# A fused attention and GLU block: scores three steps ahead, more buffers, sums stored in read order, and the A22 products later in a unit

## The chip, the cores and the metric

One core of a Trainium2 chip runs the whole program; seven cores are idle. The time is the device time of one execution in microseconds. Matrix products run on TensorE (PE in the profile), its weight loads are listed as PEld; VectorE is DVE, ScalarE is ACT, GpSimd is POOL. SyncE (SP) issues nearly all DMAs, one behind the other, from one queue in the program's order: a DMA that waits for its data holds up all that stand behind it.

## The reference

```python
mod = (_silu(c) @ w_mod).reshape(c.shape[0], 6, 1, -1)
sa, ca, ga, sb, cb, gb = (mod[:, 0], ..., mod[:, 5])
h = _layernorm(x, axis=-1) * (1 + ca) + sa
# attention: 2048 queries, 32 heads of 128, 16 pairs of key and value heads, the last 512 keys
q = (h @ wq).reshape(B, Sq, Hq, Dh)...
scores = jnp.einsum("bhqd,bhkd->bhqk", q, k) * (Dh ** -0.5)
p = _softmax(scores, axis=-1)
o = jnp.einsum("bhqk,bhkd->bhqd", p, v)
x = x + ga * (o.reshape(B, Sq, Hq * Dh) @ wo)
h = _layernorm(x, axis=-1) * (1 + cb) + sb
# gated unit: 576 -> 4608 -> 576
x = x + gb * ((_sigmoid(h @ w_gate) * (h @ w_up)) @ w_down)
```

All tensors are float32, x is 2048 x 576. Each float32 operand is split into a high part and a remainder (hi, lo), and a product is the sum of three: hi*lo, lo*hi and hi*hi.

## The kernel before, in words

The program has three stages: the Q phase (x @ wq), the attention, and what follows (output product and gated unit). The first two are one loop over steps n from -224 to 520. In a step it calls what was registered for it (`at_n`: ahead of the step's main work, `at_late`: behind it), and then the main work. In both stages every engine executes its instructions in the order in which this loop issues them.

**Q phase**, n = -224 to -1. The product is done by a seven-product scheme for 2 x 2 blocks. A unit u (32 of them) is one weight block; its seven products are named A11, A12, A22, S1, S2, S4, S3, each 7 matmuls of 128 x 512. `order` is the list of products by step and `place` its inverse. A11 and A12 of the first 14 units (EARLY) stand ahead of all; after that come five products for each early unit and seven for each later one. TensorE adds S2, S3 and A22 of a unit into the bank PA[u] (tag a, two buffers), S1 and S4 into PC[u] (tag c, one buffer). Between, ScalarE copies a bank (to gate, gate1, b), and VectorE adds such a copy to a bank to make an output (qo). So A22 of a unit can't start before VectorE has read PA[u] for the output of S3, S3 not before ScalarE has copied S2's result out (gate), and A11 of the unit after next not before A22's output has left the bank. `load_raw` fetches a unit's weights (two buffers RAW), `w_sums` builds sums on GpSimd (ws), `raw_hi`/`sum_hi` and `split_lo` the hi and lo parts (sw; sa is A22's alone) on ScalarE and VectorE. q goes to DRAM (qscr). `convert` makes the x operands of the second half. A planner places the preparation of the later stages' weights (jobs "ab", "tail", "wo", "down": loads, sums, splits, stores of x, xr, wsc, dsc, wosc) by the costs in its last line.

**Attention**, n = 0 to 511, a step for each tile of 128 queries; four tiles are a block b (one head, 512 queries), two blocks a unit of output, four units a group (one key head: two halves of the queries by two heads). In step n TensorE makes the scores of tile n + 2 (st), a quarter of the product with V for the block five steps back (ot), and the transposes of tile n's exponentials (pt). VectorE takes the negated row maximum of st (neg), ScalarE the exponential (pp) with its row sum; ScalarE copies pt (ptt, hi part) and VectorE takes the remainder (ptt, lo part). When a block's four exponentials are done, VectorE inverts the sums (rs), SP writes them to DRAM (`put_rs`, rscr<-rs), reads them back as a row for all partitions (`get_rs`, rb<-rscr), and `ov_out` multiplies ot by them into an O buffer (ov), ten steps after the block's start. `put_o` stores a unit's O buffer. For 16 of the 32 heads in the second half GpSimd adds planes of two units first (`sum_o`, `sum_last`, tile sx), and their stores come 15 and 19 steps after the last exponential instead of 9.

```python
1310         b, i = divmod(n - 5, TPB)
1314         if 0 <= n + 2 < N:
1315             scores(n + 2)
1316         if ok(b):
1317             pv(b, i)
1318         if 0 <= n < N:
1319             transp(n)
1320         if 0 <= n + 2 < N:
1321             expo(n + 2)
```

Most instructions are issued through one helper, so the profile's rows carry its line (L36); they are told apart by their tiles.

Of the kernel before, what the change touches and what calls it, by code (L numbers as in the profile page):

```python
# [9 lines left out]
F32 = mybir.dt.float32  # L10
# [6 lines left out]
P = 128  # L17
BLK = 512
TPB = BLK // P
# [25 lines left out]
def adaln_block_kernel(ctx: ExitStack, tc: tile.TileContext, x, k_cache, v_cache, wq, wo, w_gate, w_up, w_down,  # L45
                       c, w_mod, out):
    early = [True]
    nc = Ordered(tc, early, tc.nc)
    S, D = x.shape[1], x.shape[2]
    HKV, SK, DH = k_cache.shape[1], k_cache.shape[2], k_cache.shape[3]  # L50
# [3 lines left out]
    W = min(4096, max(256, SK // 4))  # L54
# [9 lines left out]
    NBLK = NB * H  # L64
# [5 lines left out]
    dram = ctx.enter_context(tc.tile_pool(name="dram", bufs=1, space=bass.MemoryType.DRAM))  # L70
# [6 lines left out]
    pools = {}  # L77
# [25 lines left out]
    def keep_order(i):  # L103
        if held[0]:
            tc.keep_in_program_order(i)
# [185 lines left out]
    NLO = -NQ  # L291
    EARLY = 14
# [36 lines left out]
    def w_hi(key, src, n=2):  # L329
        t = sw_tile([P, 5, 2, P]) if n == 2 else qw.tile([P, 5, 1, P], F32R, tag="sa", name="sa", bufs=2)  # L330
        nc.scalar.activation(t[:, 0:3], src, AF.Copy)
        HALF[key] = t, src
# [20 lines left out]
        w_hi((u, k), RAW[(u + 1) % 2][:, :, 0::2, :] if k == 2 else RAW[(u + 1) % 2][:, :, 3:4, :], 2 if k == 2 else 1)  # L353

    def sum_hi(u, k):
        w_hi((u, k), WS.pop((u, k)))

    def split_lo(u, k):
        w_lo((u, k), u, ((S1, S2), (S4, S3), (A11, A12), None, (A22,))[k])
# [180 lines left out]
    def at_n(n, fn, *args):  # L540
        at_step.setdefault(n, []).append((fn, args))
# [8 lines left out]
    for u in range(EARLY):  # L550
        order += [(u, A11), (u, A12)]
    for u in range(2 * HKV):
        if u >= EARLY:
            order.append((u, A11))
            order.append((u - 1, A22))
            order += [(u, a) for a in (S1, A12, S2, S4, S3)]
        else:
            order.append((u, S1))
            if u:
                order.append((u - 1, A22))  # L560
            order += [(u, a) for a in (S2, S4, S3)]
    order.append((2 * HKV - 1, A22))
    assert len(order) == NQ
    place = {x_: q_n(i) for i, x_ in enumerate(order)}
# [5 lines left out]
    for u in range(2 * HKV):  # L570
        if u < EARLY:
            n = place[u, S1]
            at_n(n - {0: 9, 1: 8}.get(u, 10), load_raw, u)
            sums, his = (n - 4, n - 3), {0: n - 3, 4: n - 2, 1: n - 1}
        else:
            n = place[u, A11]
            at_n(n - {EARLY: 10, EARLY + 1: 12}.get(u, 14), load_raw, u)
            sums, his = (n - 5, n - 3), {2: n - 4, 4: n - 3, 0: n - 2, 1: n}
        for k in range(2):
            at_n(sums[k], w_sums, u, k)  # L580
        for k in his:
            at_n(his[k], raw_hi if k in (2, 4) else sum_hi, u, k)
            at_n(his[k] + 1, split_lo, u, k)
# [153 lines left out]
        q_both(1, c, s, CH[c, s], nc.gpsimd if s == 1 and c not in (B11, B21, T2, T3) else nc.vector,  # L737
               bias_of(c, s) if c != B22 else None)

    for c, k in ((B11, 93), (T1, 98), (B21, 104), (T2, 106), (B22, 108), (T3, 110), (T4, 112)):  # L740
        for s in range(3):
            at_late(n + k + s // 2 + (s if c in (B11, T1) else 0), convert, c, s)
    ROOMS_FREE = n + 116
# [63 lines left out]
    def expo(n):  # L807
        b, i = divmod(n, TPB)
        half, hd, blk = blk_of(b)
        PP[n] = at.tile([P, W], F32, tag="pp", name="pp", bufs=2)  # L810
        keep_order(nc.scalar.activation(PP[n], ST.pop(n), AF.Exp, bias=NEG[b][:, i : i + 1],
                                        accum_out=SUM[b][:, i : i + 1]))
        if i == TPB - 1:
            RS[b] = at.tile([P, TPB], F32, tag="rs", name="rs", bufs=3)
            nc.vector.reciprocal(RS[b], SUM[b])
            if b < NBLK - 2:
                at_late(n - 1, put_rs, b)
                at_late(n + 2, get_rs, b)
            else:
                spread_rs(b)  # L820
                at_late(n + (0 if b == NBLK - 2 else 1), spread_mm, b)
            if last_of[half * H + hd] == b:
                m = n + (5 if b == NBLK - 1 else 9)
                if not summed(half, hd):
                    at_late(m, put_o, half, hd)
                elif hd % 2:
                    at_late(n + 8, sum_o, hd)
                    at_n(n + 15, put_sx, hd, (0, 1))
                    at_n(n + 15, put_o, half, hd - 1)
                    at_n(n + 19, put_o, half, hd)  # L830
                    at_late(n + 19, sum_last, hd)
                    at_n(n + 24, put_sx, hd, (2,))
# [28 lines left out]
    def ov_out(b):  # L861
        half, hd, blk = blk_of(b)
        unit = (half, hd)
        if unit not in OT:
            OT[unit] = pools["ov"].tile([P, TPB, 2, P], F32, tag="ov", name="ov", bufs=3)
        by_tile = RB.pop(b).rearrange("p (q i) -> p i q" if b < NBLK - 2 else "p (i q) -> p i q", i=TPB)
        nc.vector.tensor_mul(OT[unit][:, :, blk % 2, :], OP_[b].rearrange("p (i q) -> p i q", i=TPB), by_tile)
        del OP_[b]

    rscr = [dram.tile([P, TPB], F32, tag=f"rscr{i}", name=f"rscr{i}") for i in range(4)]  # L870
    oscr = [[dram.tile([P, TPB, 4, 4, P], F32, tag=f"oscr{h}_{q}", name=f"oscr{h}_{q}") for q in range(H // 8)]
            for h in range(2)]

    def put_rs(b):
        keep_order(nc.sync.dma_start(rscr[b % 4], RS[b]))

    def get_rs(b):
        RB[b] = pools["at2"].tile([P, BLK], F32, tag="rb", name="rb", bufs=2)
        keep_order(nc.sync.dma_start(RB[b], rscr[b % 4].rearrange("p t -> (p t)").partition_broadcast(P)))

    def spread_rs(b):
        DG[b] = at.tile([P, TPB, P], F32, tag="qt", name="dg", bufs=2)
# [18 lines left out]

    def sum_o(hd):
        e, o = OT[1, hd - 1], OT[1, hd]
        sx = pools["wp2"].tile([P, 2, TPB, P], F32, tag="sx", name="sx", bufs=1)
        SX[hd] = sx[:, 0], sx[:, 1], sx[:, 1], o[:, :, 0]
        pin(nc.gpsimd.tensor_add(sx[:, 0], e[:, :, 1], o[:, :, 1]))
        pin(nc.gpsimd.tensor_sub(sx[:, 1], sx[:, 0], e[:, :, 0]))
        pin(nc.gpsimd.tensor_sub(e[:, :, 1], e[:, :, 0], e[:, :, 1]))
# [33 lines left out]

    for g in range(HKV):
        n = 8 * TPB * g
        at_n(n - 13 if g else -10, load_k, g)
        at_n(n - 7 if g else -5, make_k, g)
        at_n(n - 8 if g else -4, load_v, g)
        at_n(n - 2 if g else 1, make_v, g)
    for b in range(NBLK):
        at_n(TPB * b - 13, load_qt, b)  # L950
        at_n(TPB * b - (6 if b > 1 else 5 - b), split_qt, b)

    scr = {1: dram.tile([7, P, TPB, D2], F32, tag="scr1", name="scr1")}
    xscr = [dram.tile([P, TPB, D], F32, tag=f"xscr{i}", name=f"xscr{i}") for i in range(NB)]
# [175 lines left out]
    while jobs or wide:  # L1130
        assert n < N - 44, (n, len(jobs), len(wide))

        def fits(kind):
            return [r for _, r in sorted((free[r], r) for r in SPANS if free[r] <= n and
                                         any(lo <= n and n + HOLD[kind] <= hi for lo, hi in SPANS[r]))]

        k, rooms = None, ()
        if wide and n > 40 and len(fits("wo")) > 1 and (wide[0][0] == "wo" or n > 92):
            k, rooms = wide.pop(0), fits("wo")[:2]
        elif jobs and fits(jobs[0][0]):  # L1140
            rooms = fits(jobs[0][0])[:1]
            k = jobs.pop(0)
        if due > n or k is None:
            if k is not None:
                (jobs if k[0] in ("ab", "tail") else wide).insert(0, k)
            n += 1
            continue
        kind = k[0]
        for r in rooms:
            free[r] = n + HOLD[kind]  # L1150
        at_n(n, bg_load, k, rooms)
        m = n + LEAD[kind]
        for part in range(2):
            at_n(m + (part if kind == "ab" else 2 * part), bg_sums, k, part)
            if kind != "ab":
                at_n(m + 5 + 3 * part, bg_split, k, part)
        for part in range(4 if kind == "tail" else 1):
            at_n(m + (4 if kind == "ab" else 11) + part, bg_store, k, part)
        due = max(due, n - 2) + {"ab": 8.0 if n < 0 else 5.4, "tail": 13.0 if n < 0 else 9.0}.get(kind, 7.7)

    for b in range(NB):
        at_n(max(free[b], N - 48 + 4 * b), load_x, b)
# [134 lines left out]
    for n in range(NLO, N + TPB + 5):  # L1297
        if n == 0:
            open_attention()
        if n == N - 7:  # L1300
            wctx.close()
            open_late()
        if n == N:
            early[0] = False
        while waiting and waiting[0] < n - 2:
            waiting.pop(0)
            q_store()
        for fn, args in at_step.pop(n, ()):
            fn(*args)
        b, i = divmod(n - 5, TPB)  # L1310
        if n < 0:
            q_step(*order[n - NLO])
            waiting += [n] * (len(stores) - len(waiting))
        if 0 <= n + 2 < N:
            scores(n + 2)
        if ok(b):
            pv(b, i)
        if 0 <= n < N:
            transp(n)
        if 0 <= n + 2 < N:  # L1320
            expo(n + 2)
        for fn, args in at_end.pop(n, ()):
            fn(*args)
        if n >= N - 7:
            late_step(n)
# [536 lines left out]
```

## Time and profile before

| | |
|---|---|
| runs | 3199.2 us median of 3 (3198.65 to 3200.48) |
| profiled execution | 3200.4 us, span 3198.6 us |
| Q phase | 0 to about 464 us |
| attention | about 464 to 1590 us |
| output product and gated unit | 1590 to 3198 us |
| busy share of the span | TensorE 94%, VectorE 70%, GpSimd 58%, ScalarE 57% |
| mean granted TensorE clock | 0.977 |

In a row of a group stand the engine, the operation, out<-in by tile names, the shapes, the count, then the busy time and the mean duration in ns, and behind the second bar the engine's idle time just ahead of these instructions with what ended it. In a row of waits stand the total, the number and the longest, in us. A timeline row begins with start and duration in us. SPq and ACTq are the queues that issue DMAs; the duration there is that of the issue, not of the transfer. A row of busy time by stretches gives the stretch, its length, the busy time of each engine with the number of instructions, then the granted TensorE clock, the DMA share and GB/s.

### The profile page before, as it was taken

How to read it: one execution, taken by the hardware profiler on the slowest of the kernel's cores; microseconds unless marked ns; L12 is line 12 of the kernel's file. 1: busy time of each engine (PE TensorE's matmuls, PEld its weight loads, DVE VectorE, ACT ScalarE, POOL GpSimd, SP SyncE). 2: the span in 40 equal slices, each digit the busy share in tenths (PEclk: the TensorE clock that was granted, in tenths of full speed). 3: DMA queues.
4: the chain of work that ended last, by engine and by line, in shares of the span. 5: the costliest groups of instructions: out<-in, count | busy, mean ns of one | idle time of the engine just before them, and what ended most of it. 6: DMA issues, size and time to landing. Idle time of an engine off the chain costs nothing.

```text
span 3198.6 us, 50538 instructions
## 1 busy us (share of the span) xinstructions
PE 3020.0 (94%) x16375; PEld 2572.3 (80%) x16375; DVE 2239.5 (70%) x3908; ACT 1818.8 (57%) x3663; POOL 1844.5 (58%) x1685
## 2 busy tenths in 40 slices
PE   8888988899899998889999999999999999999999
PEld 6667777677677776678799999888888888888888
DVE  6767546677677776678788877666666686666667
ACT  5455447777777776567644455444444544444443
POOL 3645544688789874432255503676665566656555
PEclk9999999999999999889999999999999999999999
DMA  5745778789888888877744865655555565555554
GB/s 172 238 160 161 233 231 225 223 256 275 260 259 289 271 250 206 234 222 219 230 184 158 311 232 170 184 159 166 171 139 147 163 192 146 146 140 146 142 138 121
DMA packets 510087, 637.28 MB, mean 199 GB/s; under 512 B 56192, under 2 KB 429824, under 8 KB 501120
## 3 DMA queue, kind: packets, MB, share of 16 engines
q1 hardware_dynamic: 508688, 633.53, 66.1%
q8 instruction: 131, 2.15, 0.3%
q14 instruction: 132, 1.08, 0.1%
q10 hardware_dynamic: 1136, 0.53, 0.1%
HBM read 426.64 MB, written 207.25 MB: 198 GB/s over the span
## 4 chain that ended last, share of the span: by engine, by line
PE 66%; DMA 9%; POOL 7%; DVE 6%; ACT 5%; issue 4%; SPq 3%; ACTq 0%; POOLq 0%; DVEq 0%
PE a L36 23%; PE w L36 12%; PE c L36 12%; PE b L36 6%; PE st L36 5%; PE ot L36 5%; SPq L36 3%; PE pt L36 3%; POOL x L36 3%; DMA rb<-rscr 3%; ACT pp L36 1%; DMA qscr<-qo 1%; DVE neg L36 1%; DVE ptt L36 1%; ACT ptt L36 1%
## 5 line engine op out<-in xcount | busy, mean ns | idle before, releaser
L36 DVE TENSOR_TENSOR x<-w,x 128x288 f32<-128x288 f32 x964 | 418.3, 450 | 239.8 <-PE w L36 236.5
L36 PE MATMUL a<-hc,sw 128*128 128x512 f32 x2016 | 584.8, 396 | 1.4 <-DVE v L36 1.3
L36 PE MATMUL ot<-ptt,vs 128*128 128x512 f32 x1536 | 456.7, 407 | 80.3 <-DVE ptt L36 79.9
L36 PE MATMUL st<-kt,qt 128*128 128x512 f32 x1536 | 497.5, 432 | 4.9 <-POOL qt L36 4.9
L36 DVE TENSOR_TENSOR ptt<-pt,ptt 128x512 fp32r<-128x512 f32 x512 | 352.3, 688 | 185.1 <-ACT ptt L36 183.8
L36 ACT ACTIVATE pp<-st,neg 128x512 f32<-128x512 f32 x512 | 351.8, 687 | 193.1 <-DVE neg L36 190.6
L36 PEld LDWEIGHTS ot<-ptt,vs 128*128 128x128 f32 x1536 | 292.8, 194 | 169.4 <-DVE ptt L36 103.8
L36 PEld LDWEIGHTS a<-hc,sw 128*128 128x128 f32 x2016 | 356.4, 188 | 41.7 <-DVE v L36 2.8
L36 ACT ACTIVATE sw<-sr 128x384 fp32r<-128x384 f32 x504 | 257.5, 519 | 190.7 <-issue 90.4
L36 ACT ACTIVATE ptt<-pt 128x512 fp32r<-128x512 f32 x512 | 304.1, 594 | 102.4 <-PE pt L36 99.4
L36 DVE TENSOR_REDUCE neg<-st 128x1 f32<-128x512 f32 x512 | 348.3, 680 | 5.8 <-PE st L36 5.5
L36 POOL TENSOR_TENSOR sw<-sr,sw 128x256 fp32r<-128x256 f32 x245 | 184.9, 755 | 281.4 <-ACT sw L36 280.5
L36 PEld LDWEIGHTS w<-wh,hl 128*128 128x128 f32 x1776 | 297.1, 188 | 52.7 <-DVE x L36 3.0
L36 PEld LDWEIGHTS pt<-ident,pp 128*128 128x128 f32 x2048 | 261.6, 144 | 84.6 <-ACT pp L36 13.3
L36 PE MATMUL w<-wh,hl 128*128 128x288 f32 x1776 | 328.2, 296 | 0.8 <-DVE x L36 0.7
L36 POOL TENSOR_TENSOR qt<-qr,qt 128x512 fp32r<-128x512 f32 x128 | 165.6, 1293 | 277.1 <-ACT qt L36 189.1
L36 PE MATMUL pt<-ident,pp 128*128 128x128 f32 x2048 | 315.5, 277 | 10.2 <-DVE ptt L36 7.9
L36 PE MATMUL c<-hc,sw 128*128 128x512 f32 x1008 | 304.0, 395 | 0.0
L36 DVE TENSOR_TENSOR sw<-sr,sw 128x256 fp32r<-128x256 f32 x259 | 187.7, 725 | 141.6 <-ACT sw L36 140.2
L36 PEld LDWEIGHTS st<-kt,qt 128*128 128x128 f32 x1536 | 258.8, 195 | 31.9 <-POOL qt L36 5.9
L36 POOL TENSOR_TENSOR hl<-vs,hl 128x512 fp32r<-128x512 f32 x139 | 191.8, 1380 | 108.5 <-ACT hl L36 106.5
L36 POOL TENSOR_TENSOR x<-x 128x288 f32<-128x288 f32 (+3 forms) x236 | 183.2, 794 | 32.6 <-ACT x L36 17.1
(299 smaller groups left out, 5864.8 us busy)
## 6 DMA issues: line engine op xcount, KB each, us to landing
sr<-wsc SPq DMA_DIRECT2D x504, 192.0 KB
wh<-dsc SPq DMA_DIRECT2D x144, 288.0 KB
qscr<-qo SPq DMA_DIRECT2D x128, 256.0 KB
qr<-qscr SPq DMA_DIRECT2D x128, 256.0 KB
vr<-oscr SPq DMA_DIRECT2D x32, 1024.0 KB
rb<-rscr SPq DMA_DIRECT2D x126, 256.0 KB
oscr<-ov SPq DMA_DIRECT2D x63, 512.0 KB
wsc<-x SPq DMA_DIRECT2D x26, 896.0 KB
```

Of the source, the lines that this page charges most:

```text
L36: i = got(*args, **kw)
```

## The change

```diff
     for u in range(2 * HKV):
-        if u >= EARLY:
-            order.append((u, A11))
+        order += [(u, a) for a in ((S1, S2, S4) if u < EARLY else (A11, S1, A12, S2, S4))]
+        if u:
             order.append((u - 1, A22))
-            order += [(u, a) for a in (S1, A12, S2, S4, S3)]
-        else:
-            order.append((u, S1))
-            if u:
-                order.append((u - 1, A22))
-            order += [(u, a) for a in (S2, S4, S3)]
+        order.append((u, S3))
...
-            at_n(n - {0: 9, 1: 8}.get(u, 10), load_raw, u)
-            sums, his = (n - 4, n - 3), {0: n - 3, 4: n - 2, 1: n - 1}
+            at_n(n - 9 if u != 1 else n - 7, load_raw, u)
+            sums, his = (n - 4, n - 3), {0: n - 3, 1: n - 1, 4: n - 1}
...
-            at_n(n - {EARLY: 10, EARLY + 1: 12}.get(u, 14), load_raw, u)
-            sums, his = (n - 5, n - 3), {2: n - 4, 4: n - 3, 0: n - 2, 1: n}
+            at_n(n - {EARLY: 8, EARLY + 1: 10}.get(u, 13), load_raw, u)
+            sums, his = (n - 5, n - 2), {2: n - 4, 0: n - 3, 4: n - 1, 1: n}
...
-        PP[n] = at.tile([P, W], F32, tag="pp", name="pp", bufs=2)
+        if n % 3 == 2 and n < N - 9:
+            PP[n] = pools["wp2"].tile([P, W], F32, tag="pp", name="pp", bufs=1)
+        else:
+            PP[n] = at.tile([P, W], F32, tag="pp", name="pp", bufs=2)
...
-            OT[unit] = pools["ov"].tile([P, TPB, 2, P], F32, tag="ov", name="ov", bufs=3)
-        by_tile = RB.pop(b).rearrange("p (q i) -> p i q" if b < NBLK - 2 else "p (i q) -> p i q", i=TPB)
+            own = b // 2 % 4 == 3 and b < NBLK - 12
+            OT[unit] = pools["wp2" if own else "ov"].tile([P, TPB, 2, P], F32, tag="ov", name="ov", bufs=1 if own else 3)
+        by_tile = RB.pop(b).rearrange("p (i q) -> p i q", i=TPB)
...
-    rscr = [dram.tile([P, TPB], F32, tag=f"rscr{i}", name=f"rscr{i}") for i in range(4)]
+    rscr = [dram.tile([TPB, P], F32, tag=f"rscr{i}", name=f"rscr{i}") for i in range(4)]
...
-        keep_order(nc.sync.dma_start(rscr[b % 4], RS[b]))
+        keep_order(nc.sync.dma_start(rscr[b % 4].rearrange("t p -> p t"), RS[b]))
...
-        sx = pools["wp2"].tile([P, 2, TPB, P], F32, tag="sx", name="sx", bufs=1)
+        sx = pools["wp2"].tile([P, 2, TPB, P], F32, tag="sx", name="sx", bufs=2)
...
-        at_n(n - 13 if g else -10, load_k, g)
-        at_n(n - 7 if g else -5, make_k, g)
+        at_n(n - 16 if g else -12, load_k, g)
+        at_n(n - 9 if g else -7, make_k, g)
...
-        at_n(TPB * b - 13, load_qt, b)
-        at_n(TPB * b - (6 if b > 1 else 5 - b), split_qt, b)
+        at_n(TPB * b - 14, load_qt, b)
+        at_n(TPB * b - (7 if b else 5), split_qt, b)
...
-        due = max(due, n - 2) + {"ab": 8.0 if n < 0 else 5.4, "tail": 13.0 if n < 0 else 9.0}.get(kind, 7.7)
+        due = max(due, n - 2) + {"ab": 12.0 if n < NLO + 97 else 8.0 if n < 0 else 5.2, "tail": 13.0 if n < 0 else 8.5}.get(kind, 7.7)
...
-        if 0 <= n + 2 < N:
-            scores(n + 2)
+        if 0 <= n + 3 < N:
+            scores(n + 3)
         if ok(b):
             pv(b, i)
+        if 0 <= n + 2 < N:
+            expo(n + 2)
         if 0 <= n < N:
             transp(n)
-        if 0 <= n + 2 < N:
-            expo(n + 2)
```

Left out are `sum_hi`, which keeps its sum, and the steps of `convert` in the second half (the last one is a step later). The sums of a block were written as four neighbouring floats for each partition; now each float goes to a row of its tile, so that the row read back has the order in which `ov_out` uses it.

TensorE in the Q phase, a later unit (bank<-x operand, weights; sa is A22), before:

```order
L36 MATMUL a<-qc,sw 128x512 x7
L36 MATMUL a<-qk,sw 128x512 x7
L36 MATMUL a<-qc,sa 128x512 x7
L36 MATMUL c<-qk,sw 128x512 x7
L36 MATMUL b<-qc,sw 128x512 x7
L36 MATMUL a<-qc,sw 128x512 x7
L36 MATMUL c<-qc,sw 128x512 x7
```

and now:

```order
L36 MATMUL a<-qc,sw 128x512 x7
L36 MATMUL a<-qk,sw 128x512 x7
L36 MATMUL c<-qk,sw 128x512 x7
L36 MATMUL b<-qc,sw 128x512 x7
L36 MATMUL a<-qc,sw 128x512 x7
L36 MATMUL c<-qc,sw 128x512 x7
L36 MATMUL a<-qc,sa 128x512 x7
```

The first row is S3 of a unit, the next A11 of the unit after. A22, which adds into the bank that S3 has just left, stood one product behind S3 and now stands five behind, with one product (S3) between it and the next A11.

SP's queue in the attention around the sums of a block (rscr<-rs writes them, rb<-rscr reads them back, qr loads the queries of a later block, the others are stores and loads of the background), before:

```order
L36 DMA rscr_341<-rs 128x4
L36 DMA qr<-qscr_9_140 128x512
L36 DMA dsc_409<-xr_4180 128x2016
L36 DMA dsc_409<-xr_4179 128x2016
L36 DMA x_112<-in_B_w_down_dram 128x288 x4
L36 DMA rb<-rscr_341 128x512
L36 DMA rscr_342<-rs 128x4
L36 DMA qr<-qscr_9_140 128x512
L36 DMA rb<-rscr_342 128x512
```

and now:

```order
L36 DMA rscr_341<-rs 128x4x1
L36 DMA dsc_409<-xr_4188 128x2016
L36 DMA dsc_409<-xr_4187 128x2016
L36 DMA x_112<-in_B_w_down_dram 128x288 x4
L36 DMA rb<-rscr_341 128x512
L36 DMA qr<-qscr_9_140 128x512
L36 DMA rscr_342<-rs 128x4x1
L36 DMA rb<-rscr_342 128x512
L36 DMA qr<-qscr_9_140 128x512
```

The write is one of 4 x 1 elements a partition instead of 4 in a row, and the qr load, which stood between the write and the read, now stands behind the read; in some blocks nothing is left between the two.

ScalarE in a few steps of the attention (pp is the exponential, ptt the copy of the transposes), before:

```order
L36 ACTIVATE qt<-qr 128x512
L36 ACTIVATE xr_4180<-xr_4179 128x1152
L36 ACTIVATE ptt<-pt 128x4x128
L36 ACTIVATE pp,sum<-st,neg 128x512
L36 ACTIVATE ptt<-pt 128x4x128
```

and now:

```order
L36 ACTIVATE qt<-qr 128x512
L36 ACTIVATE xr_4188<-xr_4187 128x1152
L36 ACTIVATE pp,sum<-st,neg 128x512
L36 ACTIVATE ptt<-pt 128x4x128
```

The exponential of a tile now stands ahead of the copy of the tile two before it, and its scores and row maximum are from the step before.

More of the change, by code (lines that the diff above doesn't have):

```diff
@@ L355, in sum_hi @@
     def sum_hi(u, k):
-        w_hi((u, k), WS.pop((u, k)))
+        w_hi((u, k), WS[u, k])
     def split_lo(u, k):
@@ L738, in convert @@
                bias_of(c, s) if c != B22 else None)
-    for c, k in ((B11, 93), (T1, 98), (B21, 104), (T2, 106), (B22, 108), (T3, 110), (T4, 112)):
+    SWK = place[HKV - 1, A11] - NLO
+    for c, k in ((B11, 93), (T1, 98), (B21, SWK), (T2, SWK + 2), (B22, SWK + 4), (T3, SWK + 6), (T4, SWK + 9)):
         for s in range(3):
@@ L874, in put_rs @@
     def put_rs(b):
-        keep_order(nc.sync.dma_start(rscr[b % 4], RS[b]))
+        keep_order(nc.sync.dma_start(rscr[b % 4].rearrange("t p -> p t"), RS[b]))
     def get_rs(b):
         RB[b] = pools["at2"].tile([P, BLK], F32, tag="rb", name="rb", bufs=2)
-        keep_order(nc.sync.dma_start(RB[b], rscr[b % 4].rearrange("p t -> (p t)").partition_broadcast(P)))
+        keep_order(nc.sync.dma_start(RB[b], rscr[b % 4].rearrange("t p -> (t p)").partition_broadcast(P)))
     def spread_rs(b):
```

## The prediction

> **What bounds the kernel now.** I read the page first, then busy time by stage, then the groups of TensorE inside the stages that the change touches, then the waits.
>
> ```profile
> span 3198.6 us, 50538 instructions
> PE 3020.0 (94%) x16375; PEld 2572.3 (80%) x16375; DVE 2239.5 (70%) x3908; ACT 1818.8 (57%) x3663; POOL 1844.5 (58%) x1685
> ```
> ```profile
> core 0: us, PE busy (x) PEld busy (x) DVE busy (x) ACT busy (x) POOL busy (x), PEclk, DMA share, GB/s
> 0.00:464.00 464.00, 414.25 (x1745) 321.31 (x1745) 295.69 (x489) 233.04 (x385) 234.10 (x247) 0.97 0.65 199
> 464.00:700.00 236.00, 206.77 (x1063) 165.80 (x1064) 164.19 (x269) 175.78 (x401) 150.68 (x147) 0.93 0.83 234
> 700.00:1163.00 463.00, 419.09 (x2201) 334.96 (x2200) 341.91 (x549) 355.57 (x777) 399.70 (x309) 0.97 0.85 268
> 1163.00:1590.00 427.00, 378.91 (x1964) 310.62 (x1963) 309.27 (x493) 279.95 (x646) 158.72 (x167) 0.93 0.78 220
> 1590.00:3198.00 1608.00, 1600.97 (x9408) 1439.66 (x9406) 1128.40 (x2110) 774.50 (x1457) 901.29 (x817) 1.00 0.56 169
> ```
>
> The first row is the Q phase, the next three the attention, the last the output product and the GLU, where TensorE does not stop. The change touches the first 1590 us alone. There TensorE is idle for 50 us in the Q phase and about 121 us in the attention, and PEclk below 1.00 says that part of the rest ran at a lower granted clock. How fast the attention could be is read where nothing waits:
>
> ```profile
> 704.71 0.95 PE L36 MATMUL st<-kt,qt 128*128 128x512 f32 x3
> 705.49 0.85 PE L36 MATMUL ot<-ptt,vs 128*128 128x512 f32 x3
> 706.18 0.60 PE L36 MATMUL pt<-ident,pp 128*128 128x128 f32 x4
> 706.54 0.95 PE L36 MATMUL st<-kt,qt 128*128 128x512 f32 x3
> ```
>
> From one st group to the next is 706.54 - 704.71 = 1.83 us: the floor of one step. 512 steps are 937 us, against 1126 us between 464 and 1590. So some 190 us are stalls, lower clock and a few products more. Where TensorE stands, and behind what:
>
> ```profile
> L36 PE MATMUL ot<-ptt,vs 128*128 128x512 f32 x1536 | 456.7, 407 | 80.3 <-DVE ptt L36 79.9
> L36 PE MATMUL pt<-ident,pp 128*128 128x128 f32 x2048 | 315.5, 277 | 10.2 <-DVE ptt L36 7.9 <-ACT pp L36 2.1 <-DVE rs L36 0.2
> L36 PE MATMUL st<-wm,ones 128*128 128x288 f32 x16 | 7.9, 584 | 14.4 <-POOL wm L36 14.3
> ACT pp L36 <- DVE neg L36: 190.6, 151, 11.4
> DVE ov L36 <- DMA oscr<-ov: 41.1, 6, 10.8
> DVE ov L36 <- DMA rb<-rscr: 34.3, 16, 6.8
> PE st L36 <- DMA kv<-in_A_k_cache_dram: 11.3, 6, 4.7
> ```
>
> TensorE waits for VectorE's ptt 80 us, and VectorE itself is held at ov: 41.1 us for an O buffer whose store has not landed, 34.3 us for the broadcast sums. One such stall, on both engines, and the clock after it:
>
> ```profile
> 1289.52 1.07 DVE L36 TENSOR_TENSOR ov<-ot,rb 128x512 f32<-128x512 f32 x1 [10.76 <-DMA oscr<-ov]
> 1291.84 1.65 PE L36 MATMUL ot<-ptt,vs 128*128 128x512 f32 x3 [10.08 <-DVE ptt L36]
> 1298.43 0.85 PE L36 MATMUL ot<-ptt,vs 128*128 128x512 f32 x3
> 1292.00:1298.00 6.00, 6.00 (x19) 4.84 (x20) 3.10 (x6) 3.24 (x9) 1.94 (x3) 0.51 1.05 320
> 1298.00:1304.00 6.00, 6.00 (x36) 5.09 (x35) 4.80 (x8) 4.36 (x11) 0.93 (x2) 1.00 0.80 183
> ```
>
> 10.76 us on VectorE become 10.08 us on TensorE (0.94 of it), and for 6 us more TensorE runs at 0.51 of its clock, 19 matmuls where 36 fit: another 3 us, 0.3 of the stall. I price a long stall at 0.94 x 1.3.
>
> **The change, part by part.** The sum goes against the profiled execution, 3200.4 us with a span of 3198.6; the median of the runs is 3199.2, 0.04% less.
>
> *Fourth O buffer.* The six waits of 41.1 us fall on the unit that takes the buffer of the late-stored head of the group before. With a buffer of its own for every fourth unit, the reuse comes at least 12 steps after the store instead of 4. What is late next is the broadcast, at one of these places already:
>
> ```profile
> 1338.93 0.39 SPq L36 DMA_DIRECT2D rscr<-rs  x1
> 1351.91 0.41 SPq L36 DMA_DIRECT2D rb<-rscr  x1
> 1359.54 1.06 DVE L36 TENSOR_TENSOR ov<-ot,rb 128x512 f32<-128x512 f32 x1 [8.73 <-DMA oscr<-ov]
> ```
>
> VectorE was free at 1359.54 - 8.73 = 1350.8, before the broadcast was even issued. If that takes some 5 us to land (my estimate; ov could start 7.2 us after it), 2.2 of these 8.7 us are won. For the stall of 10.76 us shown above:
>
> ```profile
> 1277.42 0.60 SPq L36 DMA_DIRECT2D rb<-rscr  x1
> ```
>
> landed by about 1283, VectorE idle from 1278.8: 6.5 won. That leaves 41.1 - 6.5 - 4.3 = 30 us, times 0.94 x 1.3: **-37**. Ends: -50 (all of it) and -5 (all recaptured).
>
> *Sums in read order.* ov now reads its sums with unit step. The last two blocks did so before:
>
> ```profile
> L36 DVE TENSOR_TENSOR ov<-ot,rb x128: 681/1079/1150, 493.1 to 1588.3; 128x512 f32<-128x512 f32 x128
> ```
>
> 1079 falls to 681 ns, 126 times 0.40 = 50 us of VectorE. That is not TensorE's time: per block VectorE has 4 x (688 + 680) + 1079 + 178 ns = 6.7 us of work in 4 x 1.83 = 7.3 us, so it is hidden except after a stall, while VectorE catches up. I take a fifth, **-10** (ends 0 and -20).
>
> The price is the write: 512 pieces of 4 bytes instead of 128 of 16 bytes, then read back by a DMA behind it in SP's queue. Nearest rows:
>
> ```profile
> L36 SPq DMA_DIRECT2D rscr<-rs x126: 319/412/2276, 476.2 to 1560.0; - x126
> L36 SPq DMA_DIRECT2D oscr<-ov x63: 524/525/2795, 504.4 to 1583.6; - x63
> 0.75 1.05 ACTq L36 DMA_DIRECT2D csb<-in_c_dram  x2
> 5.80 0.21 ACT L36 ACTIVATE cexp<-csb 128x5 f32<-128x5 f32 x1 [2.48 <-DMA csb<-in_c_dram]
> SPq L36 <- DMA rscr<-rs: 231.4, 81, 5.7
> SPq L36 <- POOL qt L36: 62.9, 39, 5.8
> ```
>
> Issue: oscr has 512 pieces too and takes at least 524 ns against 319, so +0.2 us. Landing: csb is the one load of 4-byte pieces, 512 of them; both its DMAs had landed 5.1 us after the first issue, beside the first loads of x. The old writes keep SP waiting up to 5.7 us. So 4-byte pieces need not be much slower; I take +0.7 us (0 to 4). The qr load, which used to stand between write and read and covered 0.4 us of the landing, now follows the read; in return the read no longer sits behind that load's waits for POOL (62.9 us). Together the broadcast comes about 1.3 us later. The 16 waits of ov for it grow by 16 x 1.3 = 20 us; I let new late blocks and the missing POOL waits cancel: **+20** (0 to +80).
>
> [...] No run here shows a 4-byte write.
>
> *Key loads three steps earlier, their transposes two.* One step more between them, 1.83 us: of the 11.3 us at most 4.7 - 1.8 = 2.9 stay. -8, times 1.3: **-10** (ends 0 and -14).
>
> *Scores three steps ahead, third pp buffer, exponential ahead of the copy.* This ends the 190.6 us in which ScalarE waits for neg, but ScalarE is not the bound; TensorE sees 10.2 us at pt, and ot still follows ptt by the same number of steps, with the copy that feeds ptt now behind an exponential. **-4** (-10 to +10). The mod products (14.3 us behind POOL) stay, as do the numbers of background pieces per stage, which the new pacing shifts by a few steps: 0. The second sx buffer: 0, because the wait of sum_last is for the store of the same sx that it overwrites.
>
> *Q phase.* A22 moves from one product behind its addition on VectorE to three (early units) or five behind it:
>
> ```profile
> L36 PE MATMUL a<-qc,sa 128*128 128x512 f32 x218 | 61.0, 420 | 22.6 <-DVE qo L36 22.3
> L36 PE MATMUL a<-qc,sw 128*128 128x512 f32 x560 | 149.8, 406 | 13.8 <-ACT gate L36 8.0 <-DVE sw L36 3.6 <-ACT qc L36 1.2
> ```
>
> sa is A22's operand: 22.3 us go. S3 gets A22 as a second product behind the gate copy, and of 8.0 us about 1 stays: -7. Times 1.3: -38. Against it, four kinds of copies on ScalarE now have one product of cover where they had two or more: A11's copy into b and A22's out of its bank (18 and 17 units), S1's copy and the fill of PA in 14 early units: 63 places. Where one product covered a copy of this kind, the gate, 32 units paid 8.0 us, 0.25 each: +16. Net **-21** (ends -38 and 0). The weight loads come one or two steps nearer their use; their buffer is also free a step later, so I put nothing down for it.
>
> Sum: -37 - 10 + 20 - 10 - 4 - 21 = -62, so 3200.4 - 62 = **3138 us**.
>
> **Rivals.** *The 4-byte write is slow* (slower than before). Five steps of 1.83 us lie between the read's place and ov, and in the row above ov started 7.2 us after the issue, in time for the broadcast: some 2 us of slack. The read already waits in 81 of 126 blocks. If the write lands x us later, ov loses 81 (x - 2) x 0.94 us. Without the put term the sum is -82, so it turns into a loss from x = 3.1; at x = 4 it would give 3200 - 82 + 152 = 3270. For it: four times the pieces, SP in order, DMA share 0.85. Against it: csb's row. [...]
>
> *The broadcast takes the O buffer's place.* If all six waits are recaptured as at 1351.91, -37 becomes -5: 3170. For it: that row. Against it: at the other places the broadcast had been issued earlier.
>
> *ScalarE's copies eat the Q phase's gain*: -21 becomes 0, 3159. For it: the gate's 8.0 us. Against it: ScalarE is busy for 233 of 464 us there.
>
> **How the numbers follow.** My sum 0.50, the broadcast 0.20 (3170), the Q phase 0.12 (3159), the slow write 0.14 (slower), all gains so small that nothing is to be told 0.04. Faster by over 0.2%, which is about what a measurement of this kernel tells from no change: 0.82; within 0.2%: 0.04; slower: 0.14. The low end, 3090, lies two thirds of the way to the sum of the good ends (-50 - 20 - 14 - 10 - 38 = -132, 3068); the high end, 3196, takes in the rivals on the near side and leaves out the slow write.
>
> **What would show it.** Right: no DVE ov wait for oscr; ov's median near 0.68 us; the idle time ahead of a<-qc,sa gone and little new ahead of b and a behind ScalarE; the first 464 us some 20 shorter and the attention some 40; SP's wait for rscr up by under 1 us a block. Wrong: SP's wait for rscr doubled and ov waiting for rb in half of the blocks; or ptt waits as long as before with rb as their cause; or a Q phase as long as before with waits for ACT qo and ACT b.

## The result and the profile after

The changed kernel takes 3984.6 us (median; 3976.0 to 3995.7) against 3199.8 us: ratio **1.245**, interval [1.242, 1.249]. The forecast was 3138 us (3090 to 3196), faster. The page of the changed kernel (its span, the engines' busy time, the granted clock in 40 slices, and the shares of the chain that ended last by engine and by line):

```profile
span 3985.7 us, 49960 instructions
PE 3209.4 (81%) x16375; PEld 2696.1 (68%) x16375; DVE 2200.4 (55%) x3908; ACT 1819.5 (46%) x3663; POOL 1845.6 (46%) x1685
...
PEclk9999987787888788777788879999999999999999
...
PE 46%; DMA 37%; SPq 6%; DVE 4%; issue 3%; ACT 2%; POOL 2%; ACTq 0%; POOLq 0%; DVEq 0%
PE a L36 19%; DMA rscr<-rs 19%; PE w L36 10%; PE c L36 10%; SPq L36 6%; DMA rb<-rscr 5%; PE b L36 5%; DMA qr<-qscr 3%; DMA wosc<-xr 1%; DMA dsc<-xr 1%; DMA dsc<-x 1%; DMA oscr<-ov 1%; PE ot L36 1%; DMA qscr<-qo 1%; DMA wsc<-xr 1%
```

The chain now runs for 19% of the span through the store of the sums. Busy time by stage (Q phase, attention, the rest; columns as in the prediction's table):

```profile
0.00:452.00 452.00, 414.61 (x1747) 325.53 (x1747) 299.63 (x488) 235.17 (x389) 239.16 (x248) 0.96 0.67 204
452.00:2380.00 1928.00, 1196.85 (x5247) 934.10 (x5246) 771.47 (x1313) 811.20 (x1821) 706.52 (x621) 0.80 0.77 143
2380.00:3985.00 1605.00, 1597.96 (x9385) 1436.47 (x9383) 1129.27 (x2108) 773.09 (x1454) 899.97 (x817) 1.00 0.56 168
```

The Q phase ends 12 us earlier, the rest is as long as before, and the attention takes 1928 us instead of 1126. TensorE stands still for 731 us of it (121 before), and the mean granted clock of the stretch is 0.80. The waits (total us, times, longest), first SyncE's queue, then VectorE and TensorE, and the group of O products:

```profile
SPq L36 <- DMA rscr<-rs: 960.7, 112, 16.4
```

```profile
DVE ov L36 <- DMA rb<-rscr: 723.9, 116, 19.1
PE ot L36 <- DVE ptt L36: 534.1, 104, 18.0
```

```profile
L36 DVE TENSOR_TENSOR ov<-ot,rb 128x512 f32<-128x512 f32 x128 | 88.5, 691 | 742.9 <-DMA rb<-rscr 723.9
```

The O product itself did get faster (1079 to 691 ns), and no wait for the O store is left. But it now waits for the broadcast in 116 of 128 blocks, and behind it TensorE waits for ptt. SyncE waits four times as long for the stored sums. Its queue in two blocks (start, duration of the issue):

```profile
1201.16 0.37 SPq L36 DMA_DIRECT2D rscr<-rs  x1
1210.80 0.32 SPq L36 DMA_DIRECT2D rb<-rscr  x1
1211.21 0.38 SPq L36 DMA_DIRECT2D qr<-qscr  x1
1211.69 0.38 SPq L36 DMA_DIRECT2D rscr<-rs  x1
...
1223.08 0.33 SPq L36 DMA_DIRECT2D rb<-rscr  x1
```

From store to read pass 9.6 and 11.4 us, and the next store goes out 0.9 us behind the first read. Over the 126 blocks the median from store to read is 12.18 us (6.35 before) and from read to next store 1.51 us (0.73 before): this queue turns once per block. From one store to the next the median is 14.5 us, while four steps of 1.83 us need 7.3.

### The profile page after: what moved, and what is told of

Read it like the earlier page. It is cut to its first block, busy times and chain, and to the rows that moved or that the text cites. A ratio compares the mean times of both kernels' runs of the same rounds, so it can differ in the third digit from the quotient of the medians.

```text
span 3985.7 us, 49960 instructions
## 1 busy us (share of the span) xinstructions
PE 3209.4 (81%) x16375; PEld 2696.1 (68%) x16375; DVE 2200.4 (55%) x3908; ACT 1819.5 (46%) x3663; POOL 1845.6 (46%) x1685
## 4 chain that ended last, share of the span: by engine, by line
PE 46%; DMA 37%; SPq 6%; DVE 4%; issue 3%; ACT 2%; POOL 2%; ACTq 0%; POOLq 0%; DVEq 0%
PE a L36 19%; DMA rscr<-rs 19%; PE w L36 10%; PE c L36 10%; SPq L36 6%; DMA rb<-rscr 5%; PE b L36 5%; DMA qr<-qscr 3%; DMA wosc<-xr 1%; DMA dsc<-xr 1%; DMA dsc<-x 1%; DMA oscr<-ov 1%; PE ot L36 1%; DMA qscr<-qo 1%; DMA wsc<-xr 1%
## 5 line engine op out<-in xcount | busy, mean ns | idle before, releaser
L36 PE MATMUL ot<-ptt,vs 128*128 128x512 f32 x1536 | 534.7, 463 | 534.4 <-DVE ptt L36 534.1
L36 PEld LDWEIGHTS ot<-ptt,vs 128*128 128x128 f32 x1536 | 336.2, 226 | 659.4 <-DVE ptt L36 584.5
L36 PE MATMUL st<-kt,qt 128*128 128x512 f32 x1536 | 558.3, 477 | 12.8 <-DVE kt L36 12.7
L36 DVE TENSOR_TENSOR ov<-ot,rb 128x512 f32<-128x512 f32 x128 | 88.5, 691 | 742.9 <-DMA rb<-rscr 723.9
L36 PE MATMUL pt<-ident,pp 128*128 128x128 f32 x2048 | 361.3, 306 | 99.0 <-DVE ptt L36 99.0
L36 PEld LDWEIGHTS pt<-ident,pp 128*128 128x128 f32 x2048 | 296.8, 161 | 199.0 <-DVE ptt L36 116.6
L36 PEld LDWEIGHTS st<-kt,qt 128*128 128x128 f32 x1536 | 296.1, 222 | 45.0 <-DVE kt L36 13.4
```

Source lines behind the costliest of these rows:

```text
L36: i = got(*args, **kw)
```

## The experiments

Ratios, with their 95% intervals, are to the kernel before on the same chip (3192 to 3196 us there); a difference in us is the ratio less 1, times 3195.

**The store alone, and all but the store.** The first puts the old storage back into the changed kernel; the second puts the new storage alone into the kernel before:

```
-    rscr = [dram.tile([P, TPB], ...
-        sync.dma_start(rscr[b % 4], RS[b])
+    rscr = [dram.tile([TPB, P], ...
+        sync.dma_start(rscr[b % 4].rearrange("t p -> p t"), RS[b])
   (only_store; after_old_store is the reverse, in the changed kernel)
```

> The changed kernel with the sums stored as before (128 pieces of 16 bytes) and read with a stride by the O product; all else of the change stays. Theory 1, the late completion of the 4-byte write is the whole loss: about 3120 us (3090 to 3150), the attention stage near 1060 us, SyncE's wait for the stored sums back from 961 to some 100 to 230 us. Theory 2, something else of the change delays the sums (three steps ahead, the key and query loads at other places in the queue): still above 3600 us, the attention stage above 1600 us.

> The kernel before with the read-order storage alone (512 pieces of 4 bytes, O product read with unit steps). Theory 1: 3800 to 4050 us, the attention stage at 1750 to 1950 us, SyncE's wait for the stored sums near 900 us, the O product near 690 ns in every block. Theory 2: within 40 us of 3199, because the rest of the change brings the loss.

Measured: only_store 3906.1 us, **1.225** [1.222, 1.228]. The store in 4-byte pieces is the loss, some 718 us of it by itself. after_old_store 3214.7 us, **1.0073** [1.0058, 1.0088]: without the store the loss is gone, but the forecast gain of some 80 us is not there either. The time lies in neither of the two expected ranges: theory 1 holds for the loss, and something else of the change cost too. Its waits:

```profile
SPq L36 <- DMA rscr<-rs: 329.2, 89, 9.2
```

```profile
DVE ov L36 <- DMA rb<-rscr: 124.8, 40, 12.4
```

With the old pieces, SyncE still waits 329 us for them (231 before), and the O product 125 us for the broadcast (34 before).

**The Q phase alone.** Only the edits to the order, the loads, the sums and the conversions:

> The kernel before with the edits of the Q phase alone (order of A22, loads and sums, conversions). The prediction's term was -21 (0 to -38); the profile of the changed kernel showed the Q phase 12 us shorter. Theory 1: 3180 to 3190 us. Rival (ScalarE's copies eat the gain): within 6 us of 3199. No store of the sums is touched, so the attention stage stays at 1126 us within 5.

Measured: 3183.3 us, **0.9978** [0.9967, 0.9988], so -7 us. The prediction's two groups of products (idle time ahead of them and what ended it):

```profile
L36 PE MATMUL a<-qc,sa 128*128 128x512 f32 x224 | 58.9, 403 | 1.2 <-DVE qo L36 1.2
L36 PE MATMUL a<-qc,sw 128*128 128x512 f32 (+1 forms) x576 | 157.3, 410 | 21.7 <-ACT a L36 8.2 <-ACT gate L36 4.4 <-DVE sw L36 3.5
```

A22's wait went, 22.6 to 1.2 us. The other group waits longer, 21.7 instead of 13.8: the gate keeps 4.4 of 8.0, and 8.2 us behind ScalarE's copies into bank a (the fills of 14 early units) are new. The trace is of the slowest of eight executions (3192.6 us); in it the first O product starts at 481.8 us instead of 493.1.

**The fourth O buffer alone.** Every fourth unit's O tile in a pool of its own:

> The kernel before with the fourth O buffer alone. The prediction's term was -37 (-50 to -5): 3150 to 3194 us, the wait of the O product for the O store (41.1 us) gone. Rival 2 (the broadcast takes the O buffer's place): 3185 to 3199 us, with the O product's wait for the broadcast grown from 34 us by 20 us or more.

Measured: 3192.1 us, **0.9994** [0.9984, 1.0004]. The wait for the O store (41.1 us) is gone, and others came:

```profile
DVE ov L36 <- DMA rb<-rscr: 54.1, 23, 7.1
PE ot L36 <- DVE ptt L36: 48.4, 31, 6.4
PE st L36 <- DMA kv<-in_A_k_cache_dram: 34.1, 9, 9.3
```

The broadcast took 20 us of it, as rival 2 had it. TensorE's wait for ptt fell from 79.9 to 48.4 us, but its wait for the keys rose from 11.3 to 34.1: a TensorE that is earlier meets the key loads. Both effects share the loss of the gain; this run alone does not divide it between them.

**Number of pieces or order?** The same store in 512 pieces but to the old order (the sums in every second float of their tile), and in 256 pieces of 8 bytes:

```
-  RS[b] = at.tile([P, TPB], ...)
+  RS[b] = at.tile([P, TPB, 2], ...)[:, :, 0]              (four_byte_old_order)
-  rscr = [dram.tile([P, TPB], ...
+  rscr = [dram.tile([2, P, 2], ...                        (eight_byte, put and read to match)
```

> The kernel before, with the reciprocals in every second float of their tile: the store is then 512 pieces of 4 bytes as in the changed kernel, but goes to the old order, where the four floats of a partition lie side by side. Theory 1a, the number of pieces makes the store late: as slow as the read-order storage alone, 3800 to 4000 us, SyncE's read issued 11 to 13 us after the store. Rival 1b, it is that a 64-byte stretch is shared by 16 partitions' pieces in read order instead of 4: within 60 us of the time before, the read issued 6 to 8 us after the store.

> The kernel before with the sums stored in two halves, 256 pieces of 8 bytes. If the lateness goes with the number of pieces: the read is issued 7.5 to 9.5 us after the store (6.35 us at 128 pieces, 12.4 us at 512), the time 3230 to 3450 us. If it goes with 4-byte pieces alone: the interval stays within 0.7 us of 6.35 and the time within 40 us of the time before.

Measured: 4035.1 us, **1.263** [1.260, 1.265], and 3372.6 us, **1.055** [1.053, 1.058]. It is the number of pieces: with the floats in the old order the store lands no earlier. That this run takes 121 us more than only_store is not divided further; its O products still read with a stride (1.06 us each). SyncE's wait in four_byte_old_order, then in eight_byte, and eight_byte's O products (shortest, median and longest, ns):

```profile
SPq L36 <- DMA rscr<-rs: 910.0, 110, 14.1
```

```profile
SPq L36 <- DMA rscr<-rs: 413.2, 101, 9.6
```

```profile
L36 DVE TENSOR_TENSOR ov<-ot,rb x128: 680/683/693, 495.6 to 1762.4; 128x512 f32<-128x512 f32 x128
```

The medians over 126 blocks of each trace, from the issue rows of store and read (the 4-piece store is that of row_only, below):

| pieces of the store | store to read, us | read to next store, us | time against before, us |
|---|---|---|---|
| 4 x 512 bytes | 4.46 | 1.96 | -32 |
| 128 x 16 (before) | 6.35 | 0.73 | 0 |
| 256 x 8 | 8.12 | 0.54 | +177 |
| 512 x 4, read order | 12.40 | 0.46 | +718 |
| 512 x 4, old order | 13.38 | 0.46 | +839 |

From store to read also holds what else stands between the two in the queue. The trace's reports of landing hold the store alone; there are 16 for each store of the kernel before. The last of them comes 3.10, 4.79, 7.15 and 11.96 us after the issue for 4, 128, 256 and 512 pieces in read order (medians; 12.56 in old order). With 512 pieces the 16 reports are spread over 6.6 us, with the old 128 over 2.0, as if the pieces landed one after the other.

About 15 ns a piece all the way by the table: 1.89 us for 124 more pieces, 1.77 for 128, 4.28 for 256; by the reports it is 14 to 19. And the sum of the two middle columns, less the floor of 7.32 us, times 126 is 169, 698 and 821 us for the last three rows: nearly the time added. The fit should not be pressed, since the kernel before has other stalls over that floor; but from 256 pieces on, SyncE's turn is what sets the block.

**Scores three ahead, and the place of the query load.** ahead_only holds the scores three ahead, the third pp buffer and the loads at their new places, with nothing else of the change. qt13 is after_old_store with one number put back, ahead13 is ahead_only with the same:

```
-        at_n(TPB * b - 14, load_qt, b)
+        at_n(TPB * b - 13, load_qt, b)
```

> The kernel before with the scores three ahead, the third buffer of exponentials and the key and query loads at their new places, nothing else. The prediction's terms: -4 and -10 us, so 3178 to 3190 on this chip's 3192. Theory 2a, after the run with the old storage (its O products waited 124.8 us for the broadcast instead of 34.3): the earlier query load stands ahead of the store in SyncE's queue and delays it; 3205 to 3230 us, and the store issued 7 to 8 us after its reciprocal instead of 3.6.

> The changed kernel with the old storage of the sums, and the query load put back to 13 steps ahead, behind the store of the sums in SyncE's queue; all else of the change stays. Theory 2a, that place is what costs: 3160 to 3185 us, the O products' wait for the broadcast back to 30 to 60 us, the store issued 3 to 5 us after its reciprocal. Rival 2b, the scores three ahead themselves or the other loads cost: 3205 to 3225 us as with the load at 14.

> The kernel before with scores three ahead, the third buffer and the early key loads, and the query load left at 13 steps. Theory 2a: the load's place alone made this part slower; now 3165 to 3192 us. Rival 2b: the scores three ahead cost by themselves, 3200 us or more.

Measured: ahead_only 3218.8 us, **1.0075** [1.0058, 1.0092]; ahead13 3174.8 us, **0.9933** [0.9917, 0.9949]; qt13 3162.6 us, **0.9901** [0.9882, 0.9921]. The one number is worth 45 us in the one pair and 55 in the other. Waits of qt13:

```profile
SPq L36 <- DMA rscr<-rs: 251.1, 81, 6.2
```

```profile
DVE ov L36 <- DMA rb<-rscr: 58.0, 24, 8.8
```

At 13 the query load is issued between store and read, while the store lands anyway. At 14 it stands between the read and the next store, and adds its issue and its own wait to SyncE's turn: from read to next store 1.50 us in after_old_store, 0.79 in qt13; the store follows its reciprocal by 7.7 us in the one and 5.5 in the other. With 6.3 us of landing and a block of 7.3 us there is no room for it.

**Two stores under way.** The read two steps later, behind the next block's store in the queue; in the changed kernel (late_get), with the query load at 13 (late_get13), and with 16-byte pieces (late16):

```
-                at_late(n + 2, get_rs, b)
+                at_late(n + 4, get_rs, b)
```

> The changed kernel, 4-byte store kept, with the read of the sums issued two steps later, behind the next block's store in SyncE's queue, so that two stores are under way at once. Theory: the loss is SyncE's series of landing and store, 12.2 + 1.5 us a block; with two under way the landing no longer sets the block, and the time falls to 3200 to 3500 us. Rival, the DMA engines themselves are held up by the 512 pieces: the landing grows as the stores overlap, and the time stays above 3800 us.

> The same with the query load put back to 13 steps ahead. If the 4-byte landing (12 us) is hidden by the two stores under way, the unit-step O product (690 ns instead of 1075) may show for the first time: 3140 to 3250 us. If the landing plus the broadcast still ends after the O product's place (8 steps of 1.83 us behind the store): 3250 to 3500 us, with the O product waiting for the broadcast in most blocks.

> The changed kernel with the old storage (16-byte pieces), the query load at 13 steps and the read two steps later, behind the next store. SyncE's wait for the stored sums should fall from 251 us to below 80. If that wait still held up the loads and stores behind it, 3135 to 3158 us against 3163 with the read at its old place; if the broadcast now comes too late for the O product, 3165 to 3200 us with its wait above 100 us.

Measured: late_get 3791.8 us, **1.187** [1.183, 1.191]; late_get13 3811.3 us, **1.193** [1.191, 1.195]; late16 3197.4 us, **1.0007** [0.9997, 1.0016]. The expectation of the first failed, and with it the theory that only the turn of the queue costs; its rival's 3800 us is nearly reached. late_get13 lies above both of its ranges. Waits of late_get:

```profile
SPq L36 <- DMA rscr<-rs: 282.6, 73, 9.7
```

```profile
DVE ov L36 <- DMA rb<-rscr: 663.8, 105, 23.2
```

SyncE waits far less (961 to 283 us), but the broadcast, issued in time, lands late: the O product starts 11.2 us after the end of its issue (4.8 in the changed kernel), and its last report comes 11.7 us after the start of the issue (5.1 there), all medians. In late16 SyncE's wait went as well (251 to 7 us), and the later read cost more than that brought: the O product waits 108 us for the broadcast instead of 58, and the time is some 34 us above that of qt13.

**A store that nobody reads.** The kernel before with a second store of the sums behind the first, in 512 or in 128 pieces, to DRAM that nothing reads:

```
+        sync.dma_start(unread[b].rearrange("t p -> p t"), RS[b])     (unread4; unread16: [P, TPB], as it lies)
```

> The kernel before, with a second store of each block's sums in 512 pieces of 4 bytes into DRAM that nothing reads, right behind the first. Theory A, the pieces hold up all transfers for as long as they land (late_get's broadcast came 11 us after its issue): 3500 us or more, the first store's read and the query loads late, though nobody waits for the new store itself. Theory B, only the reader waits for the late landing: within 60 us of the time before.

> The control: the same second store that nothing reads, in 128 pieces of 16 bytes. Theory A prices it at the old store's own share, +20 to +120 us; theory B at the issue alone, within 40 us of the time before.

Measured: unread16 3242.3 us, **1.0153** [1.0117, 1.0189]. unread4 took 3845.8 us in the execution that was traced, about 1.20, and 5939 us in the only other one. What made that one so long is open, so there is no interval and the size of the loss rests on one execution. Nobody waits for this store, and there it costs nearly as much as the one that is waited for. SyncE's queue in unread4, ScalarE's next use of the query load, and the DMA engines from 1012 to 1028 us in 40 slices of 0.4 us (busy tenths, then GB/s):

```profile
1012.33 0.40 SPq L36 DMA_DIRECT2D rscr<-rs  x1
1012.78 0.46 SPq L36 DMA_DIRECT2D unread<-rs  x1
1014.42 0.32 SPq L36 DMA_DIRECT2D qr<-qscr  x1
1024.08 0.32 SPq L36 DMA_DIRECT2D rb<-rscr  x1
```

```profile
1024.46 0.63 ACT L36 ACTIVATE qt<-qr 128x512 fp32r<-128x512 f32 x1 [5.74 <-DMA qr<-qscr]
```

```profile
DMA  9999999999999998300000000000000011479984
GB/s 380 383 380 380 377 377 366 372 374 372 375 372 370 312 278 302 118 15 0 0 0 0 0 0 0 0 0 0 0 0 0 0 61 51 169 182 213 177 128 78
```

The last of the pieces and of the query load's 128 packets starts at 1019.1 in the trace's packet records. Then the DMA engines do nothing for 5.6 us (14 slices). Only near the end of that are the store of the sums and the query load, a read from DRAM into the core, reported landed: the read that waits for the one goes out at 1024.08, ScalarE's copy of the other starts at 1024.46. So the pieces delay the report of what is issued near them: the query load, behind them in the queue, is used from 1024.46 us on, though its packets had all started by 1019.1.

The store of the sums, which stands ahead of the pieces, is late as well. Its last report comes 10.2 us after its issue in unread4 and 5.3 us in unread16 (medians of 126 blocks). The pieces of the block before had landed by then: their last report comes 11.0 us after their issue, and a block takes 13.7 us. How pieces hold up a load that was issued behind them, or a write ahead of them, no run shows.

In late_get the broadcast stands behind the next block's pieces in just this way, which would explain its late landing (11.7 us, against 5.1 in the changed kernel); a run with the broadcast on another queue was not made.

**The sums as four rows.** TensorE transposes the 128x4 reciprocals, ScalarE copies the 4x128 result out, and the store has 4 pieces of 512 bytes, in read order. row13 is the changed kernel with that and the query load at 13; row13_o3 is row13 with three O buffers; row_only is the kernel before with the 4-row store alone:

```
+        p = ps_st()
+        nc.tensor.transpose(p[:TPB, :P], RS[b], ident)
+        row = pools["wp2"].tile([TPB, P], F32, ...)
+        keep_order(nc.scalar.activation(row, p[:TPB, :P], AF.Copy))
-        keep_order(nc.sync.dma_start(rscr[b % 4].rearrange("t p -> p t"), RS[b]))
+        keep_order(nc.sync.dma_start(rscr[b % 4], row))
```

> The changed kernel with the query load at 13 steps and the sums turned into 4 rows by TensorE (one 128x4 transpose a block, some 126 x 0.3 us = 35 us of TensorE, partly in its idle time, and a copy on ScalarE) and stored as 4 pieces of 512 bytes in read order; O products read with unit steps. If the number of pieces makes the landing: the read is issued under 5 us after the store, the O product takes 690 ns, and the time is 3130 to 3175 us. If read order itself costs: the interval stays near 12 us and the time above 3600.

> The version with the sums stored as 4 rows and the query load at 13 steps, but with three O buffers as before. If the buffer pays once the sums are early, as the prediction had it (-37, ends -50 and -5): 3130 to 3150 us against 3112, with the O product waiting 40 us or more for the O store again. If it is worth nothing in any case: 3106 to 3118 us.

> The kernel before with the 4-row store in read order alone. If the 128 pieces of 16 bytes themselves cost, as the store that nothing reads says (+48 us for 128 of them): 3120 to 3165 us, the read issued 4 to 5 us after the store instead of 6.35, the O product at 690 ns. If the TensorE transposes (126 x 0.274 us) eat it: 3180 to 3215 us.

Measured: row13 3111.6 us (3107.4 to 3114.1), **0.9739** [0.9721, 0.9758], the fastest of all and below the expected 3130 to 3175; row13_o3 3117.3 us (3114.1 to 3121.1), **0.9763** [0.9748, 0.9777], in the range expected for a buffer that is worth nothing; row_only 3160.6 us, **0.9899** [0.9882, 0.9915]. Of row13, the page's head, the waits (SyncE's queue, then the others), and the transposes and O products (shortest, median, longest, ns):

```profile
span 3112.3 us, 50360 instructions
PE 3008.7 (97%) x16501; PEld 2577.4 (83%) x16501; DVE 2191.7 (70%) x3908; ACT 1836.4 (59%) x3789; POOL 1848.5 (59%) x1685
```

```profile
SPq L36 <- DMA rscr<-rrow: 133.5, 62, 6.0
```

```profile
ACT pp L36 <- DVE neg L36: 45.0, 37, 7.3
...
DVE ov L36 <- DMA rb<-rscr: 34.4, 15, 7.1
...
PE ot L36 <- DVE ptt L36: 20.9, 11, 5.9
```

```profile
L36 PE MATMUL st<-ident,rs x126: 271/273/421, 461.3 to 1472.3; 128*4 128x128 f32 x126
```

```profile
L36 DVE TENSOR_TENSOR ov<-ot,rb x128: 678/680/692, 479.6 to 1500.7; 128x512 f32<-128x512 f32 x128
```

SyncE waits 134 us for its store instead of 231. TensorE waits 21 us for ptt instead of 80, ScalarE 45 us for neg instead of 191, and TensorE's 126 transposes of 273 ns, some 34 us, are in these times. From the first O product to the last pass 1021 us, against 1095 before.

## Why the prediction was wrong, point by point

- **The step that failed: the landing of the 4-byte write**, "so 4-byte pieces need not be much slower; I take +0.7 us (0 to 4)". Measured: 12.40 - 6.35 = 6.05 us from store to read (7.2 by the reports), outside both ends. The term counted the 16 waits of ov for the broadcast; there were 116. only_store's 718 us stand against +20 for the write and -10 for the unit-step read. The row it was taken from, csb (landed 5.1 us after the first issue), is a load: its 4-byte pieces are read from DRAM and written into the core's memory. It says nothing on 4-byte writes into DRAM. The 384 more pieces of only_store cost 6.05 us, 15.8 ns each, as if they landed one after the other.
- **Rival 1 had the right mechanism, the sign and the turning point** (a loss from 3.1 us on), but its price was too small: at 6.05 us it gives 3118 + 81 x 4.05 x 0.94 = 3426 us. It counted what ov loses once per late block. Not in it was that SyncE's queue is a loop of landing, read and next store, so every microsecond over the block's 7.3 us is paid in all 126 blocks, nor that other transfers' reports wait too (in unread4 that of the store ahead of the pieces, 10.2 us instead of 5.3). Its chance, 0.14, came from csb's row.
- **The query load.** The prediction counted its new place as a give and take ("in return the read no longer sits behind that load's waits"). Measured: 45 to 55 us lost, with the old pieces.
- **Fourth O buffer, -37:** ov's wait for the O store went as forecast, the time did not: -2 alone, some -8 in row13 against row13_o3, where the intervals overlap. With the sums early little was left to win: row13_o3 waits 12.4 us for the O store. That is rival 2, near the end of -5; the broadcast took part of it, and the key loads, which the working did not name, another.
- **Unit-step read, -10:** 691 ns as forecast (681). Its worth in time was not measured by itself: row_only's -32 us hold it together with the faster landing.
- **Key loads and scores three ahead, -10 and -4:** with the query load left alone -21 (ahead13), within the ends. But it did not end "the 190.6 us in which ScalarE waits for neg": 159.1 are left in ahead13.
- **Q phase, -21:** -7. A22's wait went as forecast; ScalarE's fills of bank a, which the working priced among its 63 places, cost 8.2 us, and the gate kept 4.4 us where about 1 was assumed. That lies between the forecast and rival 3.

Of the three signs of being wrong, the first came: SyncE's wait for rscr was not doubled but four times as long, with ov waiting for rb in nine blocks of ten. The second came too, ptt's waits growing from 80 to 534 us; the third, a Q phase as long as before, did not. Put together without the 4-byte store and the moved query load, the parts give the -32 us of qt13; the prediction's terms for them add up to -72.

## What to carry to other kernels

Count the pieces of every small write to DRAM before its bytes (the last report of these 2 KB came after 3.10 us with 4 pieces, 11.96 with 512), and price it from a write, not from a load; where values must change their order, turn them on the core, as TensorE did here (273 ns a block in row13, and row_only took 32 us less than before), so that the store has long pieces. Where one queue stores, waits and reads back once per block, add up that turn and hold it against the block: here its medians added up to 7.1 of 7.3 us before the change, and a load moved to the wrong side of the store cost 1.4 to 1.7%. A slow write that nobody waits for wasn't free here either (about 1.20 in the traced execution of unread4): what was issued near it was reported late, the store of the sums after 10.2 us instead of 5.3.

## What the runs showed of the hardware

- The 2 KB store of the sums to DRAM was reported landed 14 to 19 ns later for each piece (last report after 3.10, 4.79, 7.15, 11.96 us for 4, 128, 256, 512 pieces, medians), though its packets start early: those of the changed kernel's store at 2328.76, with nothing queued behind it, 1.4 to 2.6 us after the issue, and its read goes out 9.45 us after it. Why each piece takes that long no run shows.
- In unread4 the query load behind 512 such pieces was reported late, the DMA engines idle meanwhile (its packets started by 1019.1, it was used from 1024.46 us on). The store issued ahead of the pieces was reported late as well (after 10.2 us, against 5.3 with 128 pieces behind it in unread16).
- The O product on VectorE took 683 ns with its second operand read at a stride of 8 bytes (eight_byte), as with unit step (680 in row13, 691 in the changed kernel); at a stride of 16 bytes it took 1079 (before). What makes the difference no run shows.
